# One weight load, two small copies, one scaling and two later steps at the start of a fused RWKV and feed-forward kernel

## The chip, the cores and the metric

The kernel runs on one core of a Trainium2 chip. The metric is the device time of one execution in microseconds (us); the time before is the median of three runs. The engines of the core work side by side, each through its own list of instructions in a fixed order: TensorE (PE, matrix products into the PSUM banks), VectorE (DVE), ScalarE (ACT), GpSimd (POOL) and SyncE (SP). They wait for each other through semaphores. Loads that convert float32 to bfloat16 are issued by POOL and share one software queue; SP and ACT issue others on hardware queues.

## What is computed

A recurrence with a decaying state per head (4 sequences, 8 heads, 768 tokens, head width 48), then a feed-forward layer with a leaky ReLU over all 3072 tokens:

```python
for t in range(S):
    cur = np.einsum('bhd,bhe->bhde', u[None] * kt, vt)
    y[:, :, t] = np.einsum('bhd,bhde->bhe', rt, state + cur)
    state = w[None, :, :, None] * state + np.einsum('bhd,bhe->bhde', kt, vt)
...
h = x @ w_in                      # 384 -> 2048
g = np.maximum(0.01 * h, h)
out = g @ w_out                   # 2048 -> 384
```

## The kernel before

**Tiling.** The tokens are cut into 24 tiles of 128; tile n belongs to sequence n % 4 in a permuted order, so tiles 0 to 3 open the four sequences and have no incoming state. Inside a tile the recurrence is a masked product. Powers of the decay, counted from the middle of the tile, are put into two tables (`qtab` for r, `ktab` for k), so that a scaled r and a scaled k give the weights of all token pairs as one product per head. The state goes from a tile to the next tile of its sequence through `wl`, the decay over 128 tokens.

**Order.** The string `ORDER` (line 29) lists all steps by name; `run` calls them one after the other, and each appends instructions to its engine's list. So the order of two names matters only where both put work on the same engine, where a step reads what another wrote, and where PSUM banks are handed out: `take()` gives the bank that has been free longest in the list's order, `give()` returns one. `Sched` turns the reads and writes of each step into semaphore waits.

**Names used below**, with n the tile:

- Loads: `rn`, `kn`, `vn` are the tile's r, k and v (line 268, POOL, 96 KB in bfloat16); r0 and k0 alone come as float32 over SP and ACT into `r_f` and `k_f` (line 249). `wi0` to `wi3` are the quarters of w_in (line 278, POOL, 384 KB), `wo0` to `wo3` those of w_out (line 282).
- The start: `bc` spreads w over all partitions on PE (line 379, needs the `w_row` load), `lnw`, `qtab`, `ktab` (lines 386, 393, ACT) make the tables; `c0q@`, `c0k@` (line 485, DVE) copy r0 and k0 as bfloat16 into `raw`; `T0q`, `T0k` turn `raw` on PE; `Cu` (line 634, PE) puts w*u by columns into a PSUM bank and `C` (`decay_columns`, line 645) copies it into `wu` in two instructions; `W` (`decay_table`, line 654, ACT) fills `wl` in two instructions.
- A tile: `Pnq`, `Pnk` scale r and k by the tables (`prep_half`, line 431, DVE, into `qk`), `Tnq`, `Tnk` turn them on PE (line 500) and `tnq`, `tnk` bring them back into `tp` on ACT (line 518). `An` is the product for all token pairs (line 529, PE), `Mna`, `Mnb` mask it into `at` on DVE (line 559, from tile 4 on line 563). `Xn` (line 452, DVE) multiplies turned r and k, `Dn` (line 578, PE) sums it with `wu`, `Qn` scales v by that sum (line 459, DVE); from tile 4 on `qn` (lines 466 to 470, DVE) and `Qn` (line 477, POOL) do this in another way. `Yn` (lines 712 and 719, PE) is the tile's output and `yn` (line 733, ACT) copies it into `xT`.
- The state: `Kn` (line 604, PE) is the tile's k-v product, `Sn` (`state`, line 661; line 677 for tiles 0 to 3, DVE) multiplies it by `wl` into the state and gives the bank back.
- The layer: `Gn.f` (line 758, PE) is a quarter of h for tile n, quarter f needing `wif`; `gn.f` (line 769, ACT) is the leaky ReLU; `J`, `j` are the same for two tiles at once; `Hn` (line 782, PE) and `hn` (line 794, ACT) give the output. `F2`, `F4` (line 315) are matmuls whose result nobody reads.

PE's list around the change is: bc, T0q, T0k, Cu, F2, U, A0, T1q, D0, T1k, F4, T3k, K3, A1, D1, Y0, T3q, K0, G0.1, Y1, A3, T2q, D3, G1.1, T2k, G0.3, G1.3, Y3, A2, T4q, T5k, G3.1, G3.3, G3.2, D2, G0.2, T5q, K2, T4k, G1.2.

Of the kernel before, what the change touches and what calls it, by code (L numbers as in the profile page):

```python
# [6 lines left out]
ALU = mybir.AluOpType  # L7
AF = mybir.ActivationFunctionType
# [4 lines left out]
B, H, S, D = 4, 8, 768, 48  # L13
# [5 lines left out]
E = 64  # L19
NP = H // 2  # L20
# [5 lines left out]
TURNED, DIAG, CARRY, EXACT, RAW = 6, 4, 4, 1, 1  # L26
STRIPS = 8
SWAP = 12
ORDER = """
w8 qk0 k0 v0z one r0 trow ones v0y tcol wlz r1 id8 wi1 u8 zr table Cw Wl id E w bc lnw c0q@ T0q c0k@ tri u exps k1 T0k  # L30
u16 wu8 Cu t0q t0k qtab P1q F2 k3 v3 U A0 ktab T1q v0 t1q X0 C D0 P1k T1k t1k F4 M0b P3k M0a T3k K3 utab X1 A1 D1 Q0
Y0 t3k P0k r3 P3q v1 M1a T3q r2 y0 k2 K0 M1b Q1 P2q W G0.1 Y1 t3q X3 wi3 A3 y1 g0.1 S3 T2q D3 G1.1 g1.1 k5 t2q r5 r4
P2k T2k wi2 S0 v2 M3b t2k Q3 G0.3 g0.3 G1.3 k4 M3a Y3 P5k A2 y3 P4q T4q v4 wi0 T5k v5 wo3 t4q g1.3 G3.1 q5 t5k Q5 G3.3
g3.3 P5q r6 wo2 X2 g3.1 M2b wo1 G3.2 D2 Q2 G0.2 g0.2 T5q t5q K2 P4k T4k M2a t4k S2 G1.2 g3.2 q4 Q4 K1 S1 Y2 A5 A4 G1.0
y2 G2.1 M5a G0.0 G2.3 M4a M5b Y5 g0.0 y5 M4b Y4 y4 G2.2 g2.2 K4 J2.4 j2.4 k6 wo0 J2.1 J2.2 g1.0 g1.2 S4 k7 P6q q6 j2.1
P6k P7k G2.0 r7 q7 X6T J2.6 j2.6 J2.3 j2.3 k8 G3.0 J2.7 j2.7 k9 r9 j2.2 J2.5 P7q g3.0 g2.3 X7T J2.0 H1 h1 r8 g2.0 Q6
# [26 lines left out]
class Sched:  # L63
# [7 lines left out]

    def add(self, eng, emit, R=(), W=(), dma=None):
        o = Op()
        o.eng, o.emit, o.dma, o.inc, o.val = eng, emit, dma, False, None
        deps = []
        for key in R:
            w = self.writer.get(key)
            if w is not None:
                deps.append((w, True))
        for key in W:  # L80
            w = self.writer.get(key)
            if w is not None:
                deps.append((w, False))
            for r in self.readers.get(key, ()):
                deps.append((r, False))
        o.deps = []
        for d, raw in deps:
            if d.dma is None and d.eng == eng and dma is None and (eng == "pe" or not raw):
                continue
            if d is not o and d not in o.deps:  # L90
                o.deps.append(d)
        for key in R:
            self.readers.setdefault(key, []).append(o)
        for key in W:
            self.writer[key] = o
            self.readers[key] = []
        self.ops.append(o)
        return o
# [47 lines left out]
def bass_rwkv5_eagle__then__act_leaky_relu_kernel(  # L146
# [13 lines left out]
    def SB(name, shape, dt=BF16):  # L160
        return ctx.enter_context(nc.sbuf_tensor(name, shape, dt))
# [15 lines left out]
    wu = SB("wu", [128, NP, 2])  # L177
    prod = [SB(f"prod{i}", [128, NP, 128]) for i in range(4)]
    lnw = SB("lnw", [128, HD], FP32)
# [3 lines left out]
    qtab = SB("qtab", [128, HD])  # L183
    ktab = SB("ktab", [128, HD])
    tcol = SB("tcol", [128, 1], FP32)
    trow = SB("trow", [128, 2, 128], FP32)
    turned = SB("turned", [128, 2 * NP, 128])
    raw = SB("raw", [128, 2 * H, E])
# [3 lines left out]
    ones = SB("ones", [128, 128])  # L192
# [10 lines left out]
    qk = [SB(f"qk{i}", [128, 2 * H, E]) for i in range(NQK)]  # L203
# [11 lines left out]
    V, A, PE, SP, G = nc.vector, nc.scalar, nc.tensor, nc.sync, nc.gpsimd  # L215
    sch = Sched(ctx, nc)
    add = sch.add
# [6 lines left out]
    def give(key):  # L224
        free.append(key[1])
# [9 lines left out]
    def swapped(n):  # L235
        return n >= SWAP and n % 2 == 0

    def loaded(which, n):
        return [(which, n, 0), (which, n, 1)] if swapped(n) else [(which, n)]
# [11 lines left out]
    def load_one(n, which, pace=()):  # L251
# [6 lines left out]
        if swapped(n):  # L258
# [5 lines left out]
            dst = both.rearrange("p n (h e) -> p (n h) e", h=H)[:, :, 0:D]  # L264
            add("pool", lambda: G.dma_start(dst, src), R=pace, W=[(which, n0, half), (which, n0 + 2, half)],
                dma=f"{which}{n}")
            return
        add("pool", lambda: G.dma_start(dst, src), R=pace, W=[(which, n)], dma=f"{which}{n}")  # L268

# [40 lines left out]
    def fill(n):  # L310
# [7 lines left out]

        add("pe", emit, R=["ones"], W=[("ps", i), f"fill{n}"])

# [101 lines left out]
    def hd(x):  # L422
        return x.rearrange("p (h d) -> p h d", d=D)

    def k_of(n):
        return k_sb[:, slot(n), :] if n >= EXACT else k_f[:, n, :]

    def r_of(n):
        return r_sb[:, slot(n), :] if n >= EXACT else r_f[:, n, :]

    def prep_half(n, half):
        iq = n % NQK
        src, tab, name, done = ((r_of(n), qtab, "r", "qp"), (k_of(n), ktab, "k", "kp"))[half]
        named = "qk"[half] + "tab"
        if swapped(n):
            tab, named = (qtab_s, ktab_s)[half], named + "_s"
        add("dve", lambda: V.tensor_tensor(qk[iq][:, H * half:H * half + H, 0:D], hd(src), hd(tab[:, :]), ALU.mult),  # L437
            R=loaded(name, n) + [named, ("qk0", iq)], W=[(done, iq)])

    def turn_dma(n):  # L440
        iq = n % NQK
# [3 lines left out]
    def prep(n):  # L445
        prep_half(n, 0)
        prep_half(n, 1)
        turn_dma(n)
# [196 lines left out]
    def decay_columns():  # L645
        ps_c, key = c_bank["u"]
        for hh in range(2):
            rows = slice(64 * hh, 64 * hh + D)
            add("dve", lambda rows=rows, hh=hh: V.tensor_copy(
                wu[rows, :, hh:hh + 1].rearrange("p m o -> p (m o)"), ps_c[rows, 0:NP]),  # L650
                R=[key, "wu"], W=[f"wu{hh}"])
        give(key)

# [134 lines left out]
    def g2_out(n, c0=0, c1=HD):  # L788
# [7 lines left out]
        if swapped(n):  # L796
# [12 lines left out]
            W=["w_row"], dma="w"),  # L809
# [7 lines left out]
        "bc": spread_w, "lnw": log_w, "qtab": lambda: table(qtab, tcol, "q", "tcol"),  # L817
        "ktab": lambda: table(ktab, kexp, "k", "kexp"), "Cw": w_columns, "Cu": wu_columns, "E": turned_table,
        "Wl": log_columns, "C": decay_columns, "W": decay_table,
        "u16": u_cast, "U": u_spread, "utab": u_table,  # L820
        "ts": swapped_times, "tris": swapped_triangle,
# [4 lines left out]
    }  # L826
    stage = {
        "P": lambda n, x: prep_half(n, half_of[x]), "T": lambda n, x: turn_mm(n, half_of[x]),
        "t": lambda n, x: turn_out(n, half_of[x[0]], "dve" if x[1:] else "act"),
        "X": lambda n, x: turn_dma(n) if x else diag(n), "A": lambda n, x: a_mm(n), "B": lambda n, x: a_pair(n),  # L830
# [82 lines left out]
```

## Time and profile before

| | |
|---|---|
| median of 3 runs | 167.31 us (166.94 to 167.38) |
| the profiled execution | 166.78 us, its span 165.0 us |
| PE busy | 157.4 us, 95% |
| DVE busy | 105.5 us, 64% |
| ACT busy | 90.4 us, 55% |
| POOL busy | 109.5 us, 66% (issuing loads is counted here) |
| DMA | 20.21 MB, mean 123 GB/s |

Times in the rows below are us from the span's start. A row of the chain of waits gives start, length and the work that set the end; a row of a timeline gives start, length, engine, line, operation, what it writes and reads, how many instructions were merged, and in brackets the idle time before it with what ended it. Instructions of one engine overlap by about 0.1 us in the timelines, so the chain's lengths are the ones to add up. A row of DMA issues ends with the kilobytes and the median us from issue to landing.

### The profile page before, as it was taken

What the parts mean: (1) busy time and instruction counts of PE and PEld (TensorE: products, weight loads), DVE (VectorE), ACT (ScalarE), POOL (GpSimd) and SP (SyncE); (2) the same over time, 40 slices, a digit from 0 to 9 for tenths busy, and PEclk for the clock granted to TensorE, in tenths of its full rate; (3) what the DMA queues carried; (4) which work ended last, traced back from release to release, by engine and by line L of the source; (5) the groups of instructions that cost most, each with busy time, mean ns of one, the idle gap of its engine ahead of it and who ended that gap; (6) DMA issues with size and microseconds to landing.
All of it is one profiled execution on the core that took longest, in us unless ns stands there. A gap on an engine that the chain in (4) does not pass through costs nothing.

```text
span 165.0 us, 5331 instructions
## 1 busy us (share of the span) xinstructions
PE 157.4 (95%) x2303; PEld 119.7 (73%) x2303; DVE 105.5 (64%) x254; ACT 90.4 (55%) x170; POOL 109.5 (66%) x125
## 2 busy tenths in 40 slices
PE   0899999999999999999999999999999999999994
PEld 0487899985568678668668678678678668678663
DVE  7798998269378699948939939939939933000000
ACT  3856883865168339347447447438438439449121
POOL 8999798987999969999199399299380270000000
PEclk9999999999999999999999999999999999999999
DMA  7999999999999999999939959959980630020023
GB/s 110 149 141 158 169 189 190 181 150 154 149 153 202 121 118 137 158 208 130 160 90 113 145 134 94 163 132 81 104 192 4 127 97 3 4 61 34 17 82 97
DMA packets 101365, 20.21 MB, mean 123 GB/s; under 512 B 94555, under 2 KB 101342, under 8 KB 101342
## 3 DMA queue, kind: packets, MB, share of 16 engines
q0 software_dynamic: 76512, 10.03, 93.2%
q1 hardware_dynamic: 23790, 9.65, 29.8%
q8 instruction: 18, 0.29, 0.8%
q10 hardware_dynamic: 1040, 0.20, 0.6%
q14 instruction: 5, 0.04, 0.1%
HBM read 20.45 MB, written 4.72 MB: 153 GB/s over the span
## 4 chain that ended last, share of the span: by engine, by line
PE 91%; ACT 2%; DVE 2%; DMA 2%; SPq 1%; issue 0%; ACTq 0%
PE ps L782 38%; PE ps L758 37%; PE ps L719 6%; PE ps L529 2%; PE ps L500 2%; DMA w_row<-in_w_dram 2%; PE ps L548 1%; PE ps L595 1%; PE ps L604 1%; PE ps L315 1%; ACT xT L733 1%; DVE at L559 1%; PE ps L379 1%; DVE st L677 1%; PE ps L712 1%; ACT out_sb L794 0%
## 5 line engine op out<-in xcount | busy, mean ns | idle before, releaser
L758 PE MATMUL ps<-xT,w_in_sb 128*128 128x256 bf16 (+1 forms) x672 | 66.2, 257 | 0.2
L782 PE MATMUL ps<-w_out_sb,gT 128*128 128x384 bf16 (+2 forms) x400 | 64.6, 320 | 0.0
L769 ACT ACTIVATE gT<-ps 128x512 bf16<-128x512 f32 x96 | 56.3, 598 | 14.8 <-PE ps L758 10.9
L758 PEld LDWEIGHTS ps<-xT,w_in_sb 128*128 128x128 bf16 x672 | 57.2, 98 | 6.6 <-ACT xT L733 0.5
L477 POOL TENSOR_TENSOR at<-ident,s_tok 128x512 bf16<-128x512 bf16 x40 | 42.1, 1081 | 24.8 <-DVE s_tok L470 24.7
L782 PEld LDWEIGHTS ps<-w_out_sb,gT 128*128 128x128 bf16 x400 | 38.1, 98 | 23.1
L794 ACT ACTIVATE out_sb<-ps 128x384 f32<-128x384 f32 (+2 forms) x25 | 11.8, 478 | 45.3 <-PE ps L782 45.3
L563 DVE CAST_PREDICATED at<-mask,ps 128x512 bf16<-128x512 uint16 x28 | 17.8, 685 | 4.7 <-PE ps L529 4.6
L563 DVE CAST_PREDICATED at<-mask_s,ps 128x512 bf16<-128x512 uint16 x12 | 7.7, 687 | 16.1 <-PE ps L548 16.1
L268 POOL DMA_DIRECT2D v_sb<-in_v_dram x18 | 16.3, 920 | 0.0
L268 POOL DMA_DIRECT2D r_sb<-in_r_dram x17 | 15.7, 928 | 0.1
L268 POOL DMA_DIRECT2D k_sb<-in_k_dram x17 | 15.6, 924 | 0.0
L468 DVE TENSOR_TENSOR rku<-r_sb,ku 128x384 bf16<-128x384 bf16 x20 | 12.2, 611 | 0.7
L733 ACT ACTIVATE xT<-ps 128x384 bf16<-128x384 f32 x24 | 10.8, 491 | 2.7 <-PE ps L719 2.6
L470 DVE TENSOR_REDUCE s_tok<-rku 128x8 f32<-128x384 bf16 x20 | 11.1, 553 | 0.7
L719 PE MATMUL ps<-at,v_sb 128*32 128x128 bf16 x384 | 10.8, 223 | 0.0
L719 PEld LDWEIGHTS ps<-tp,st 128*32 128x32 bf16 x240 | 7.2, 96 | 3.0 <-issue 2.9
L719 PEld LDWEIGHTS ps<-at,v_sb 128*32 128x32 bf16 x384 | 8.8, 98 | 0.5 <-issue 0.2
L719 PE MATMUL ps<-tp,st 128*32 128x128 bf16 x240 | 9.1, 221 | 0.0
L671 DVE TENSOR_TENSOR sum_t<-ps,st 64x192 bf16<-64x192 f32 x24 | 8.5, 354 | 0.6
L466 DVE TENSOR_TENSOR ku<-k_sb,u_tab 128x384 bf16<-128x384 bf16 x20 | 7.0, 352 | 2.0 <-DMA k_sb<-in_k_dram 1.8
L437 DVE TENSOR_TENSOR qk<-k_sb,ktab 128x384 bf16<-128x384 bf16 x17 | 7.5, 443 | 1.1 <-DMA k_sb<-in_k_dram 1.0
(82 smaller groups left out, 119.9 us busy)
## 6 DMA issues: line engine op xcount, KB each, us to landing
out_dram<-out_sb SPq DMA_DIRECT2D x17, 192.0 KB, 3.3
v_sb<-in_v_dram POOLq DMA_DIRECT2D x24, 96.0 KB, 5.1
r_sb<-in_r_dram POOLq DMA_DIRECT2D x23, 96.0 KB, 4.5
k_sb<-in_k_dram POOLq DMA_DIRECT2D x23, 96.0 KB, 5.3
w_in_sb<-in_moe_w_in_dram POOLq DMA_DIRECT2D x4, 384.0 KB, 6.3
w_out_sb<-in_moe_w_out_dram POOLq DMA_DIRECT2D x4, 384.0 KB, 7.5
out_dram<-out_sb SPq DMA_DIRECT2D x12, 96.0 KB, 2.2
tp<-qk SPq DMA_TRANSPOSE x18, 4.5
```

Of the source, the lines that this page charges most:

```text
L268: add("pool", lambda: G.dma_start(dst, src), R=pace, W=[(which, n)], dma=f"{which}{n}")
L468: add("dve", lambda: V.tensor_tensor(rku[i2][:, :], r_of(n), ku[i2][:, :], ALU.mult), R=loaded("r", n) + [("ku", i2)], W=[("rku", i2)])
L470: add("dve", lambda: V.tensor_reduce(s_tok[i2][:, :], hd(rku[i2][:, :]), AX.X, ALU.add), R=[("rku", i2)], W=[("s", i2)])
L477: add("pool", lambda hh=hh, s_of=s_of: G.tensor_tensor(at[ia][:, hh, :, :], ident[:, :].unsqueeze(1).to_broadcast([128, NP, 128]), s_of.un ...
L563: add("dve", lambda: V.copy_predicated(at[n % NAT][:, hh, :, :], tri[:, :].bitcast(mybir.dt.uint16).unsqueeze(1).to_broadcast([128, NP, 12 ...
L671: add("dve", lambda part=part: V.tensor_tensor(both[part], kv[part[0]], st[n % NT][part], ALU.add), R=[key, ("st", n % NT)], W=[("sum", n ...
L719: last = PE.matmul(ps_y[32 * q:32 * q + 32, 128 * s:128 * s + 128], a, m, start=not whole and step == 0, stop=step == len(columns[q]) - 1)
L733: add("act", lambda: A.activation(xT[ix][:, :, 128 * slot:128 * slot + 128], ps_y[:, 0:HD].rearrange("p (s t) -> p s t", t=128), AF.Copy), ...
L758: last = PE.matmul(ps_g[:, step * f:step * f + step], w_in_sb[:, s, 128 * fb:128 * fb + 128], xT[ix][:, s, t], start=s == 0, stop=s == NSL ...
L769: add("act", lambda: A.activation(gT[ig][:, fb0:fb0 + count, t], ps_g[:, :].rearrange("p (f t) -> p f t", t=128 * width), AF.Prelu, alpha= ...
L782: last = PE.matmul(ps_o[:, 0:c1 - c0], gT[ig][:, s, 128 * slot:128 * slot + 128], w_out_sb[:, s, c0:c1], start=s == 0, stop=s == NFB - 1)
L794: add("act", lambda: A.activation(out_sb[io][:, c0:c1], ps_o[:, 0:c1 - c0], AF.Copy), R=[key], W=held)
```

## The change

- `wi1` is issued behind `v0` in place of ahead of `k1`, so POOL's list begins r1, k1, k3, v3, v0, wi1, r3 in place of r1, wi1, k1, k3, v3, v0, r3.
- `C` is done by ACT in place of DVE, and stands behind `ktab` in place of behind `X0`; its bank is free that much earlier in the list.
- `P0k` reads k of tile 0 from `raw` (bfloat16) in place of `k_f` (float32).
- `W` stands behind `t3q` in place of ahead of it, on ACT.
- `S0` stands behind `M3a` in place of ahead of `M3b`, on DVE.

The lists of PE and SP keep their order.

```diff
-w8 qk0 k0 v0z one r0 trow ones v0y tcol wlz r1 id8 wi1 u8 zr table Cw Wl id E w bc lnw c0q@ T0q c0k@ tri u exps k1 T0k
-u16 wu8 Cu t0q t0k qtab P1q F2 k3 v3 U A0 ktab T1q v0 t1q X0 C D0 P1k T1k t1k F4 M0b P3k M0a T3k K3 utab X1 A1 D1 Q0
-Y0 t3k P0k r3 P3q v1 M1a T3q r2 y0 k2 K0 M1b Q1 P2q W G0.1 Y1 t3q X3 wi3 A3 y1 g0.1 S3 T2q D3 G1.1 g1.1 k5 t2q r5 r4
-P2k T2k wi2 S0 v2 M3b t2k Q3 G0.3 g0.3 G1.3 k4 M3a Y3 P5k A2 y3 P4q T4q v4 wi0 T5k v5 wo3 t4q g1.3 G3.1 q5 t5k Q5 G3.3
+w8 qk0 k0 v0z one r0 trow ones v0y tcol wlz r1 id8 u8 zr table Cw Wl id E w bc lnw c0q@ T0q c0k@ tri u exps k1 T0k u16
+wu8 Cu t0q t0k qtab P1q F2 k3 v3 U A0 ktab C T1q v0 wi1 t1q X0 D0 P1k T1k t1k F4 M0b P3k M0a T3k K3 utab X1 A1 D1 Q0
+Y0 t3k P0k r3 P3q v1 M1a T3q r2 y0 k2 K0 M1b Q1 P2q G0.1 Y1 t3q W X3 wi3 A3 y1 g0.1 S3 T2q D3 G1.1 g1.1 k5 t2q r5 r4
+P2k T2k wi2 v2 M3b t2k Q3 G0.3 g0.3 G1.3 k4 M3a S0 Y3 P5k A2 y3 P4q T4q v4 wi0 T5k v5 wo3 t4q g1.3 G3.1 q5 t5k Q5 G3.3
...
-        add("dve", lambda: V.tensor_tensor(qk[iq][:, H * half:H * half + H, 0:D], hd(src), hd(tab[:, :]), ALU.mult),
-            R=loaded(name, n) + [named, ("qk0", iq)], W=[(done, iq)])
+        src, reads = (raw[:, H * half:H * half + H, 0:D], [("raw", half)]) if n < RAW else (hd(src), loaded(name, n))
+        add("dve", lambda: V.tensor_tensor(qk[iq][:, H * half:H * half + H, 0:D], src, hd(tab[:, :]), ALU.mult),
+            R=reads + [named, ("qk0", iq)], W=[(done, iq)])
...
-            add("dve", lambda rows=rows, hh=hh: V.tensor_copy(
-                wu[rows, :, hh:hh + 1].rearrange("p m o -> p (m o)"), ps_c[rows, 0:NP]),
+            add("act", lambda rows=rows, hh=hh: A.activation(
+                wu[rows, :, hh:hh + 1].rearrange("p m o -> p (m o)"), ps_c[rows, 0:NP], AF.Copy),
                 R=[key, "wu"], W=[f"wu{hh}"])
```

## The prediction

> **What bounds the kernel now.** I read the page first, then the whole chain of waits, then the timelines of PE, DVE, ACT and POOL over the first 25 us, and last the DMA issues in short windows, one load at a time.
>
> ```profile
> span 165.0 us, 5331 instructions
> ...
> PE 91%; ACT 2%; DVE 2%; DMA 2%; SPq 1%; issue 0%; ACTq 0%
> ```
>
> PE carries the span, so only time in which PE waits can be won, and any new wait of PE is paid in full. All edits lie before 20 us. The chain of waits there:
>
> ```profile
> 5.12 1.01 PE ps L379 x4
> ...
> 12.66 0.58 PE ps L719 x15
> ...
> 13.27 0.49 ACT xT L733
> 13.76 0.24 ACT wl L657
> ...
> 14.41 0.61 ACT tp L518
> ...
> 15.04 0.42 DVE prod L452
> 15.46 0.47 DVE st L677
> 15.93 0.27 DVE qk L437
> 16.20 0.47 DVE st L677
> 16.67 0.60 DVE at L559
> 17.26 0.46 DVE vs L459
> 17.73 0.61 DVE at L559
> ...
> 18.38 0.34 PE ps L712 x3
> 18.73 0.34 PE ps L719 x16
> ...
> 19.94 2.01 PE ps L758 x36
> ...
> 23.21 0.38 PE ps L500 x4
> ```
>
> Three stretches. From 5.12 to 13.24 all pieces are PE's, back to back (the rows left out are PE's too): no other engine can give anything there. From 13.27 to 18.38 the chain leaves PE: y0, W and t3q on ACT, then X3, S3, P2k, S0, M3b, Q3, M3a on DVE, and PE's Y3 starts when M3a ends. From 18.38 on it is PE again, up to the tail.
>
> **The change part by part.** The order of PE's own instructions stays the same; what moves is on POOL, DVE and ACT.
>
> *The two copies of C.* They leave DVE and go to ACT behind ktab:
>
> ```profile
> 4.66 0.17 ACT L642 ACTIVATE wcol<-ps 128x4 f32<-128x4 f32 x1 [2.21 <-PE ps L623]
> ...
> 9.43 1.19 ACT L518 ACTIVATE tp<-ps 128x512 bf16<-128x512 f32 x2 [1.07 <-PE ps L500]
> ```
> ```profile
> 8.58 0.35 DVE L649 CAST wu<-ps 48x4 bf16<-48x4 f32 x2
> ...
> 11.62 0.55 DVE L437 TENSOR_TENSOR qk<-k_f,ktab 128x384 bf16<-128x384 f32 x1
> ...
> 15.85 0.35 DVE L437 TENSOR_TENSOR qk<-k_sb,ktab 128x384 bf16<-128x384 bf16 x1
> ```
>
> ACT's nearest row is L642, the same four columns out of PSUM: 2 x 0.17 = 0.34 us, laid into the 1.07 us that ACT idles before t1q at 9.43. Without that cover t1q, t1k and utab behind it would be 0.34 us late. DVE is freed of 0.35 us. *P0k* reads bfloat16 in place of float32: 0.55 becomes 0.35, as in the bfloat16 row, so 0.20 us less. Both savings, 0.55 us, fall before Y0 at 12.66, in the stretch where PE waits for nobody, and M1a behind them waits for A1 from PE. I take 0; the ends are 0 and, were DVE the limit at y0, -0.55.
>
> *W behind t3q, S0 behind M3a.* T3q ran before y0, so t3q can follow y0 directly: 13.76 to 14.37. X3 needs P2q, over at 14.4: 14.4 to 14.8. W follows t3q with its two instructions, 0.6 to 0.7 us in the chain, to 15.0, well ahead of y1 at 15.2, which waits for Y1 and is not delayed. S3 now waits for W: DVE stands from 14.8 to 15.0 with P2k, M3b, Q3 and M3a queued behind it. From 15.0 the chain's own steps give S3 15.5, P2k 15.75, M3b 16.35, Q3 16.8, M3a 17.4, then S0 17.9 (its bank is asked for next at G3.3, after 20). So M3a ends some 0.9 us earlier than 18.34. PE can't use all of it:
>
> ```profile
> 16.66 1.50 PE L758 MATMUL ps<-xT,w_in_sb 128*128 128x128 bf16 x24
> ```
>
> G0.3 and G1.3 are 24 matmuls of 2.01/36 = 0.056 us: PE is through at 18.0. Y3 moves from 18.38 to 18.0: **-0.38 us at this place**.
>
> *What is late next.* DVE goes on with P5k and P4q; T4q on PE (19.32) needs P4q, T4k (23.21) needs P4k.
>
> ```profile
> 18.24 0.35 DVE L437 TENSOR_TENSOR qk<-k_sb,ktab 128x384 bf16<-128x384 bf16 x1
> 18.68 0.36 DVE L437 TENSOR_TENSOR qk<-r_sb,qtab 128x384 bf16<-128x384 bf16 x1
> ...
> 20.47 1.27 DVE L452 TENSOR_TENSOR prod<-tp 128x512 bf16<-128x512 bf16 x1
> ...
> 22.72 0.34 DVE L437 TENSOR_TENSOR qk<-k_sb,ktab 128x384 bf16<-128x384 bf16 x1
> ```
> ```profile
> 1.41 1.07 POOL L268 DMA_DIRECT2D r_sb<-in_r_dram  x1
> 2.47 0.77 POOL L278 DMA_DIRECT2D w_in_sb<-in_moe_w_in_dram  x1
> 3.20 1.82 POOL L268 DMA_DIRECT2D k_sb<-in_k_dram  x2
> 4.99 1.83 POOL L268 DMA_DIRECT2D v_sb<-in_v_dram  x2
> ...
> 9.41 0.92 POOL L268 DMA_DIRECT2D k_sb<-in_k_dram  x1
> ...
> 11.93 1.78 POOL L268 DMA_DIRECT2D r_sb<-in_r_dram  x2
> ```
>
> The second load of the 11.93 row is r4, issued at 12.8. Its time to landing, and below it those of r1 (issued at 1.41), v0 (5.9), k2 (9.41) and, for comparison, of a load issued at 112.4 in a train on a queue that had been empty:
>
> ```profile
> r_sb<-in_r_dram POOLq DMA_DIRECT2D x1, 96.0 KB, 5.9
> ```
> ```profile
> r_sb<-in_r_dram POOLq DMA_DIRECT2D x1, 96.0 KB, 4.0
> ```
> ```profile
> v_sb<-in_v_dram POOLq DMA_DIRECT2D x1, 96.0 KB, 4.9
> ```
> ```profile
> k_sb<-in_k_dram POOLq DMA_DIRECT2D x1, 96.0 KB, 4.2
> ```
> ```profile
> k_sb<-in_k_dram POOLq DMA_DIRECT2D x1, 96.0 KB, 3.7
> ```
>
> r4 lands at 12.8 + 5.9 = 18.7, and P4q starts at 18.68: **P4q waits for the load already**, if only for the 0.1 us after P5k. From there DVE has no gap to P4k (ku, rku, the reduction, P5q, X2, M2b, Q2, P4k), which ends at 23.06, and PE's T4k starts at 23.21, behind it. So an earlier Y3 is lost again by T4k: if r4 lands when it did, T4k stays at 23.21 and the gain of 0.38 us is worth 0. If r4 is late by d, T4k is late by d, and PE after it has nothing to give it back.
>
> *wi1 behind v0* decides d. All these loads share the software queue, in POOL's order. From v0's landing (10.8) to k2's (13.6) four loads land: 0.70 us each while there is a backlog; POOL issues one in 0.9 us. Before, wi1's big transfer stood second (landed at about 8.1, 2.65 us after r1 at 5.4) and made that backlog at once. After, k1, k3, v3, v0 are issued at 2.47, 3.4, 4.3, 5.2 and wi1 at 6.1, r3 at 6.8 as before. **Lower end:** the queue never runs dry; v0 lands at 5.4 + 4 x 0.70 = 8.2, wi1 at 10.85, where v0 landed before: d = 0. **Upper end:** each lands 3.7 after its issue as at 112.4; v0 at 8.9, wi1 2.65 later at 11.55: d = 0.7. r1's 4.0 is far nearer to 3.7 than to the 4.9 of a backlog, so I take d = 0.5, in the upper half. (wi1 itself, at 11.5, is in time for G0.1 at 13.81; wi3 and wi0 move by d as well and stay ahead of G0.3 and G1.0 until d passes about 0.5 and PE's own delay.)
>
> The Trainium skill, "DMA: Bandwidth & Descriptors", section "Anatomy of one DMA", prices a load of POOL's queue at about 2.0 us plus its bytes over 436 GB/s, 2.2 us for 96 KB. By that rule r4 would be there at 15, the order on the queue would not matter and the 0.38 us would stay won. The trace does not agree: 5.9 us for r4.
>
> **Sum** against the profiled execution (span 165.0, 166.78 us with what lies around it): 0 for C and P0k, -0.38 and +0.38 for W and S0, +0.5 for wi1: 167.3. The median shown, 167.31, is 0.53 above that execution, so the forecast is 167.31 + 0.5 = **167.8 us**, its own range 167.4 to 168.1.
>
> **The rivals.** *r4 stops being late* (the other side). Place: P4q. For it: r4 was late by only 0.1 us, its 5.9 us are 1.7 more than k2's 4.2, and a load that takes the backlog better would be there by 18.4. Then Y3's 0.38 us stay, less what P4q costs: T4q needs it 0.6 us earlier than 19.04. With 0.2 us more from a front that starts earlier because w_row (landed before 5.12) no longer shares the engines with wi1: 167.31 - 0.38 - 0.2 = 166.7. It decides from r4 landing at 18.3 or earlier. Against it: nothing ahead of r4 in the queue gets smaller, only the order changes.
>
> *The queue runs dry at every load.* The train's 3.7 us grow, or POOL's issues stretch as r1's 1.07 did: d of 0.7 to 1.0. wi3 (landed at 10.28 + 5.8 = 16.1 before) then comes after 16.66 too, but that stall and T4k's are one and the same delay: 167.31 + 0.85 = 168.2.
>
> *PE's pace.* The sixteen L719 matmuls take 0.58 at 12.66 and 0.34 at 18.73: PE doubles its pace near 13.2. If the changed stretch moves that point by some 3.4 us, the work between at half pace is worth 1.7 us either way: 165.6 or 169.0. Against it: PE's order and its unbroken stretch from 5.12 stay. The Trainium skill, "TensorE: Matmul & The Clock Gate", Part 1, has the gate judge free-running windows of 3.4 us, by which the phase, not this change, would move it; the halved pace agrees with the rows.
>
> *C on ACT delays D0.* wu is ready at 8.37 + 0.34 = 8.7, D0 runs at 9.19: not given a chance of its own.
>
> **How the numbers follow.** This kernel's measurement tells 0.3%, 0.5 us, from no change: 166.8 to 167.8. Forecast 0.46, its centre on the upper bound: 0.24 slower, 0.22 same. Queue dry at every load 0.26: slower 0.25. r4 in time 0.22: faster 0.16, same 0.06. Pace 0.06: half each side. That is faster 0.19, same 0.29, slower 0.52. The range 166.6 to 168.5 holds the first three cases and leaves out the pace and the tails.
>
> **What would show it.** DVE's row for P4q with an idle ahead of it put down to the r_sb load, at 19.0 to 19.3, and r4's landing 6.2 to 6.5 us after its issue: the forecast's main step. Y3 near 18.0 and M3a's end near 17.4: the W and S0 step. T4q after 19.4 and T4k at 23.5 to 23.9. P0k at 0.35, and the copies on ACT at 0.17 each inside its idle. k1 to v0 landing one every 0.9 us rather than every 0.7 would show the dry queue; 0.7 would refute it. The prediction is wrong if r4 lands at 18.7 or earlier, if T4k starts before 23.2, or if PE's pace doubles elsewhere than at 13.2.

## The result and the profile after

| | before | after |
|---|---|---|
| median in one comparison, 22 runs each | 166.93 us | 167.68 us |
| ratio after/before | | 1.0037, 95% interval 1.0021 to 1.0054 |
| the profiled execution | 166.78 us, span 165.0 us | 166.92 us, span 165.1 us |

The ratio and its interval leave out one far slower execution of each kernel (232.94 us of before, 169.94 us of after). By that ratio the change makes the kernel slower by 0.37%, some 0.6 us (0.0037 x 166.93); the two medians lie 0.75 us apart. The profiled execution of after is one of its fastest: of the 22 runs of after only one, at 166.82 us, is shorter. So its trace shows where the time is decided, but not the whole of the loss.

The chain of waits of after (start, length, what set the end), from the first loads to T4k:

```profile
1.40 1.07 POOL r_sb L268
2.47 1.77 POOL k_sb L268 x2
4.24 1.80 POOL v_sb L268 x2
6.04 0.74 POOL w_in_sb L278
...
11.96 0.82 POOL r_sb L268
12.78 6.10 DMA r_sb<-in_r_dram
...
18.90 0.04 DVE qk L438
...
23.43 0.38 PE ps L501 x4
```

Before, this chain was PE's from 5.12, left it at y0 and came back at Y3 (18.38). Now it is POOL's list of load issues up to 12.78, then r4's 6.10 us to landing, then P4q at 18.90 and DVE without a gap to T4k. Nothing that PE, ACT or DVE does before 18.9 stands in it. T4k starts at 23.43, 0.22 us later than before; behind it the span is the same (165.1 - 23.43 = 141.7 us, before 165.0 - 23.21 = 141.8 us).

The timeline of DVE in after, the rows of P0k, P3q, M3a, S0, P5k and P4q (in brackets the idle time ahead and what ended it):

```profile
11.33 0.35 DVE L438 TENSOR_TENSOR qk<-raw,ktab 128x384 bf16<-128x384 bf16 x1
12.22 0.36 DVE L438 TENSOR_TENSOR qk<-r_sb,qtab 128x384 bf16<-128x384 bf16 x1 [0.54 <-DMA r_sb<-in_r_dram]
...
16.56 0.69 DVE L560 TENSOR_TENSOR at<-ps,mask 128x512 bf16<-128x512 f32 x1
17.16 0.55 DVE L678 TENSOR_TENSOR st<-ps,wl 128x384 bf16<-128x384 f32 x1
17.62 0.35 DVE L438 TENSOR_TENSOR qk<-k_sb,ktab 128x384 bf16<-128x384 bf16 x1
18.90 0.36 DVE L438 TENSOR_TENSOR qk<-r_sb,qtab 128x384 bf16<-128x384 bf16 x1 [0.93 <-DMA r_sb<-in_r_dram]
```

DVE is done with P5k at 17.97, 0.6 us earlier than before, and then stands 0.93 us for r4. It also stands 0.54 us for r3, at P3q.

The timeline of ACT: the two copies of C, t1q and t1k, and W behind t3q; and the timeline of PE: Y0's matmuls, Y3 and T4q:

```profile
8.36 0.35 ACT L650 ACTIVATE wu<-ps 48x4 bf16<-48x4 f32 x2
9.36 1.13 ACT L519 ACTIVATE tp<-ps 128x512 bf16<-128x512 f32 x2 [0.65 <-PE ps L501]
...
13.28 0.59 ACT L519 ACTIVATE tp<-ps 128x512 bf16<-128x512 f32 x1
13.75 0.74 ACT L658 ACTIVATE wl<-wcol 48x192 bf16<-48x192 f32 x2
```
```profile
12.43 0.41 PE L720 MATMUL ps<-at,v_sb 128*32 128x128 bf16 x16
...
17.82 0.33 PE L713 MATMUL ps<-ident,vs 128*128 128x128 bf16 x3
...
19.32 0.62 PE L501 MATMUL ps<-ident,qk 128*128 128x128 bf16 x8 [0.50 <-DVE qk L438]
```

C fills part of ACT's idle time (1.07 us before, 0.65 left). PE takes 0.41 us for the sixteen matmuls of Y0, where before took 0.62, so it doubled its pace near 12.4 in this execution and near 13.2 in before's. It was 0.17 us ahead there besides (12.43, before 12.60), and y0 follows 0.38 us earlier (12.89, before 13.27). Y3 starts at 17.82 in place of 18.38. T4q starts at 19.32, as before: PE finished early and waits 0.50 us for P4q.

The loads, from the view of DMA issues of after, one load at a time (last number: us from issue to landing): k1 (issued at 2.46), v0 (5.06), wi1 (6.03), r3 (6.75), k2 (9.40) and r4 (12.78):

```profile
k_sb<-in_k_dram POOLq DMA_DIRECT2D x1, 96.0 KB, 3.9
...
v_sb<-in_v_dram POOLq DMA_DIRECT2D x1, 96.0 KB, 4.5
...
w_in_sb<-in_moe_w_in_dram POOLq DMA_DIRECT2D x1, 384.0 KB, 5.4
...
r_sb<-in_r_dram POOLq DMA_DIRECT2D x1, 96.0 KB, 5.4
...
k_sb<-in_k_dram POOLq DMA_DIRECT2D x1, 96.0 KB, 4.9
...
r_sb<-in_r_dram POOLq DMA_DIRECT2D x1, 96.0 KB, 6.1
```

Issue and time added give the landing. k1 is there at 6.4 in place of 8.8. But k2 lands at 14.3, where before it landed at 13.6 (9.41 + 4.2): 0.6 us late, with the same loads ahead of it.

What the queue moved meanwhile, from the view of DMA between 8.0 and 8.5 us, first before, then after (packets, MB, mean rate):

```profile
DMA packets 745, 0.07 MB, mean 140 GB/s; under 512 B 745, under 2 KB 745, under 8 KB 745
```
```profile
DMA packets 101, 0.02 MB, mean 39 GB/s; under 512 B 90, under 2 KB 101, under 8 KB 101
```

All these packets are the software queue's. From 4.5 to 8.0 us, with k1 to v0 on it, after moved 105 GB/s; with 96 KB loads in a backlog (8.5 to 11 us) before moved 141. So the queue is short of work in after until wi1 comes, though never without a packet under way.

### The profile page after: what moved, and what is told of

It is laid out like the page before. It is cut to its first block, busy times and chain, and to the rows that moved or that the text cites. A ratio compares the mean times of both kernels' runs of the same rounds, so it can differ in the third digit from the quotient of the medians.

```text
span 165.1 us, 5331 instructions
## 1 busy us (share of the span) xinstructions
PE 157.2 (95%) x2303; PEld 119.6 (72%) x2303; DVE 105.1 (64%) x252; ACT 90.5 (55%) x172; POOL 109.5 (66%) x125
## 4 chain that ended last, share of the span: by engine, by line
PE 84%; POOL 7%; DMA 4%; DVE 2%; ACT 1%; issue 1%; POOLq 0%; ACTq 0%
PE ps L783 38%; PE ps L759 36%; PE ps L720 5%; DMA r_sb<-in_r_dram 4%; POOL r_sb L268 2%; POOL k_sb L268 2%; POOL v_sb L268 2%; PE ps L549 1%; PE ps L530 1%; PE ps L596 1%; POOL w_in_sb L278 1%; DVE prod L453 1%; PE ps L605 1%; ACT xT L734 1%; ACT out_sb L795 0%
## 5 line engine op out<-in xcount | busy, mean ns | idle before, releaser
L770 ACT ACTIVATE gT<-ps 128x512 bf16<-128x512 f32 x96 | 56.3, 598 | 15.0 <-PE ps L759 11.1
L795 ACT ACTIVATE out_sb<-ps 128x384 f32<-128x384 f32 (+2 forms) x25 | 11.8, 478 | 45.3 <-PE ps L783 45.3
L564 DVE CAST_PREDICATED at<-mask,ps 128x512 bf16<-128x512 uint16 x28 | 17.8, 685 | 4.9 <-PE ps L530 4.7
L564 DVE CAST_PREDICATED at<-mask_s,ps 128x512 bf16<-128x512 uint16 x12 | 7.7, 687 | 16.1 <-PE ps L549 16.1
L268 POOL DMA_DIRECT2D r_sb<-in_r_dram x17 | 15.8, 936 | 0.1
L469 DVE TENSOR_TENSOR rku<-r_sb,ku 128x384 bf16<-128x384 bf16 x20 | 12.2, 612 | 0.7
L734 ACT ACTIVATE xT<-ps 128x384 bf16<-128x384 f32 x24 | 10.8, 491 | 2.4 <-PE ps L720 2.3
L471 DVE TENSOR_REDUCE s_tok<-rku 128x8 f32<-128x384 bf16 x20 | 11.1, 553 | 0.7
```

Source lines behind the costliest of these rows:

```text
L469: add("dve", lambda: V.tensor_tensor(rku[i2][:, :], r_of(n), ku[i2][:, :], ALU.mult), R=loaded("r", n) + [("ku", i2)], W=[("rku", i2)])
L471: add("dve", lambda: V.tensor_reduce(s_tok[i2][:, :], hd(rku[i2][:, :]), AX.X, ALU.add), R=[("rku", i2)], W=[("s", i2)])
L564: add("dve", lambda: V.copy_predicated(at[n % NAT][:, hh, :, :], tri[:, :].bitcast(mybir.dt.uint16).unsqueeze(1).to_broadcast([128, NP, 12 ...
L734: add("act", lambda: A.activation(xT[ix][:, :, 128 * slot:128 * slot + 128], ps_y[:, 0:HD].rearrange("p (s t) -> p s t", t=128), AF.Copy), ...
L770: add("act", lambda: A.activation(gT[ig][:, fb0:fb0 + count, t], ps_g[:, :].rearrange("p (f t) -> p f t", t=128 * width), AF.Prelu, alpha= ...
L795: add("act", lambda: A.activation(out_sb[io][:, c0:c1], ps_o[:, 0:c1 - c0], AF.Copy), R=[key], W=held)
```

## The experiments

The theory: moving wi1 leaves the software queue without a backlog while k1 to v0 come in; the time lost there is a delay d of all later loads; r4 is among them and releases P4q. The rivals: the loss belongs to the other four edits (C, P0k, W, S0); r4 stops being late; the queue runs dry at every load; the point at which PE doubles its pace has moved. All edits below that only move names in `ORDER` are shown by the part of the list that they change. Each median stands beside that of the kernel before from the same comparison, in brackets.

**After once more, unchanged.**

> The changed kernel once more, for a second profile. Theory A (the load of r4 is late because w_in's first quarter stands behind v0; P4q waits for it, and all after T4k is late by that): P4q starts at 18.8 to 19.3 behind an idle put down to the r_sb load, T4k at 23.4 to 23.8, time 1.002 to 1.006 of before. Rival B (the copies on ACT, W or S0 cost the time, the loads' order costs nothing): the same time, but T4k no later than before's 23.21 and a wait elsewhere.

Median 167.26 us (before 167.11), ratio 1.0013, interval 0.9987 to 1.0039. Its chain of waits:

```profile
12.79 6.01 DMA r_sb<-in_r_dram
...
23.36 0.38 PE ps L501 x4
```

The chain is the same, with r4 a little earlier. The ratio's interval holds 1 as well as 1.0037: twelve runs don't settle 0.4% here, and the main reading below rests on two kernels, wi1's move alone and the other four edits alone, each measured twice.

**wi1's move alone, twice** (the kernel before, with this edit only):

```diff
-r1 id8 wi1 u8 ... T1q v0 t1q
+r1 id8 u8 ... T1q v0 wi1 t1q
```

> Before, with w_in's first quarter behind v0 and nothing else changed. Theory A: r4 lands at 18.9 (6.1 us after its issue, 5.9 before), P4q starts there, T4k at 23.4 in place of 23.21, time 1.002 to 1.005. Rival B: T4k at 23.2 and time 1.000 within 0.001.

> The same kernel as in the run with w_in's first quarter moved alone, once more, since a single profile scatters: r4 landed at 18.7 to 20.2 in the profiles so far, and T4k came 4.54 us after P4q whenever P4q waited for r4, the end 141.7 us after T4k. Theory A: 1.002 to 1.006 of before again, P4q behind r4. If the first time was scatter: 1.000 within 0.002.

Medians 167.66 us (before 167.11), ratio 1.0044, interval 1.0012 to 1.0075; and 167.62 us (167.14), 1.0032, 1.0009 to 1.0055. The chain of waits of the first, and the timeline of DVE of the second:

```profile
12.78 7.09 DMA r_sb<-in_r_dram
...
19.89 0.04 DVE qk L437
...
24.43 0.38 PE ps L500 x4
```
```profile
13.03 0.36 DVE L437 TENSOR_TENSOR qk<-r_sb,qtab 128x384 bf16<-128x384 bf16 x1 [0.84 <-DMA r_sb<-in_r_dram]
...
19.93 0.36 DVE L437 TENSOR_TENSOR qk<-r_sb,qtab 128x384 bf16<-128x384 bf16 x1 [1.15 <-DMA r_sb<-in_r_dram]
```

The move alone costs as much as the whole change. r4 lands 7.1 us after its issue in both, r3 is late too (P3q stands 0.84 us in the second), and T4k starts 4.54 us behind P4q, as it does in after (23.43 - 18.90 = 4.53). Both profiled executions (168.00 and 168.48 us) are slower than the medians. From 8.0 to 8.5 us the queue moved 44 and 46 GB/s in them, and 89 in after once more.

**The other four edits alone, twice** (after, with wi1 put back):

```diff
-r1 id8 u8 ... T1q v0 wi1 t1q
+r1 id8 wi1 u8 ... T1q v0 t1q
```

> After, with w_in's first quarter back in its old place: C, P0k, W and S0 alone. Theory A: Y3 at 17.8 to 18.0 in place of 18.38, but r4 still lands at 18.7, so DVE idles 0.4 to 0.8 us ahead of P4q, T4k stays at 23.2 and the time at 0.999 to 1.001. Rival B: 1.003 to 1.005, as after. A third way, the gain of 0.38 us stays: 0.997 to 0.998 with T4k at 22.8.

> The same kernel as in the run with all edits but the load, once more. Theory A: 0.998 to 1.001 of before, since r4 (or, ahead of it, k1, which then lands after 8.8) holds DVE and not the steps that became shorter. If those steps gain by themselves: 0.997 or less.

Medians 166.89 us (before 167.11), ratio 0.9998, interval 0.9966 to 1.0029; and 167.01 us (167.14), 0.9991, 0.9961 to 1.0021. C, P0k, W and S0 change nothing that can be measured here (the intervals reach 0.3% to 0.4% to either side). From 8.0 to 8.5 us the queue moved 140 GB/s in both, as in before. The two profiles lie far apart. The chain of waits of the first, then that of the second:

```profile
12.77 7.44 DMA r_sb<-in_r_dram
...
20.24 0.04 DVE qk L438
...
24.78 0.39 PE ps L501 x4
```
```profile
17.06 1.34 PE ps L759 x24
18.40 0.17 PE ps L713 x3
...
22.96 0.36 PE ps L501 x4
```

In the first, r4 took 7.44 us and T4k came at 24.78, later than in after; yet of its 12 runs, the profiled one (168.19 us) is the second slowest, and the median is below before's. In the second, r4 was there at 18.4, P4q waited only 0.15 us for it, and the chain is PE's: T4k at 22.96. One kernel, 1.8 us between two executions: *a single profile of this kernel can't size d.*

The landings of the loads show more. Each is the time of issue (POOL's timeline) plus the time to landing of that load:

| wi1 stands | kernel | v0 | wi1 | r3 | k2 | wi3 | r5 | r4 |
|---|---|---|---|---|---|---|---|---|
| second | before | 10.8 | 8.0 | 11.5 | 13.6 | 16.1 | 18.3 | 18.7 |
| second | the other four edits | 11.1 | 8.3 | 11.8 | 13.9 | 16.8 | 19.6 | 20.2 |
| second | the same, again | 10.8 | 8.0 | 11.5 | 13.6 | 15.5 | 18.0 | 18.4 |
| behind v0 | after | 9.6 | 11.5 | 12.2 | 14.3 | 16.2 | 18.4 | 18.9 |
| behind v0 | after once more | 8.5 | 11.1 | 11.8 | 13.9 | 15.8 | 18.2 | 18.8 |
| behind v0 | wi1's move alone | 9.7 | 12.0 | 12.8 | 14.8 | 16.8 | 19.3 | 19.9 |
| behind v0 | the same, again | 9.1 | 12.3 | 13.0 | 15.6 | 17.6 | 19.0 | 19.9 |
| behind k1 | see below | 11.2 | 9.2 | 12.0 | 14.0 | 16.0 | 18.3 | 18.7 |

Read the table by columns. At k2 the order shows on average: with wi1 second k2 lands at 13.6 to 13.9 (mean 13.7), with wi1 behind v0 at 13.9 to 15.6 (mean 14.6). Single executions can touch: after once more has k2 as early as the latest with wi1 second. Three kernels below have one of these two orders up to k2 as well: before without wi3 has k2 at 14.2; after with r4 ahead of k5 and after without wi3 have it at 15.0 and 14.8. Behind k2 each execution adds something of its own: wi3 lands 1.9 to 2.9 us behind k2, and r5 another 1.4 to 2.9 us behind wi3. That scatter is larger than d, and both end at P4q.

**r4 issued ahead of k5** (after, otherwise unchanged):

```diff
-wi3 A3 y1 g0.1 S3 T2q D3 G1.1 g1.1 k5 t2q r5 r4
+wi3 A3 y1 g0.1 S3 T2q D3 G1.1 g1.1 r4 k5 t2q r5
```

> After, with r4 issued ahead of k5 and r5 in place of behind them. Theory A: r4 lands near 17, P4q follows P5k at about 18.0 with no idle, T4q at 18.8, T4k at 22.6 to 22.9; then w_in's quarter wi0, which lands at 25.2, is the next bound (G1.0 at 25.3 in place of 25.65), so some 0.3 us less than after: 0.999 to 1.001 of before. If r4 is not what holds the stretch: T4k at 23.4 and the time of after, 1.004.

Median 167.31 us (before 167.11), ratio 1.0004, interval 0.9972 to 1.0036. In its chain of waits r4 is gone, but r3 stands there, and PE is slow for long:

```profile
6.75 6.24 DMA r_sb<-in_r_dram
...
17.05 0.54 PE ps L501 x4
...
18.48 0.22 PE ps L501 x4
...
24.61 0.30 PE ps L501 x4
```

Four matmuls of L501 take 0.54 us at 17.05 and 0.22 us at 18.48. So PE doubled its pace between the two, near 17.8 in this execution, where before did it near 13.2, with one and the same order on PE. What r4 gave, r3 and the pace took: T4k at 24.61. The median is what theory A expected, the path is not, and this execution (168.11 us) is the third slowest of its 12.

**wi3 not loaded, in after and in before.** wi3 is struck from `ORDER`, and the products of the fourth quarter read the second quarter's weights in place, so the output is another:

```diff
+at0 = 128 * (fb if fb // 4 != 3 else fb - 8)
...
-R=[("xT", ix, slot) for slot in slots] + [("win", fb0 // 4)],
+R=[("xT", ix, slot) for slot in slots] + [("win", fb0 // 4 if fb0 // 4 != 3 else 1)],
```

> After, without the load of w_in's quarter wi3; its products take quarter 1 instead, so the matmuls are the same in number and size and the output is another. 2.5 us of transfer ahead of r4 and r5 in the queue are gone. Theory A (r4 holds the stretch): r4 lands near 16.4, P4q follows P5k near 18.0 without a wait, T4k moves to 22.5 to 22.8, wi0 lands 2.5 us earlier and holds nothing, time 0.995 to 0.997 of before. If the loads are not the limit: T4k at 23.4, time 1.003.

> Before, without the load of wi3, in the same way. Theory A: r4 is there early, so M3a (18.33) and the rest of DVE's list hold the stretch: P4q at 18.5 to 18.6, T4k at 23.0 to 23.1, time 0.998 to 1.000, so 0.3 to 0.6 us behind the kernel of after without wi3: the gain of C, P0k, W and S0 that the late load hides. If those steps bring nothing by themselves: the same time as after without wi3.

After without wi3: 166.89 us (before 167.07), ratio 0.9998, interval 0.9970 to 1.0027. Before without wi3: 166.85 us, 0.9981, 0.9953 to 1.0010. Neither differs from before, and the gain that was expected did not show. In both the wait for r4 went away, as the timelines of DVE say (the first, P3q and P4q; the second, P1k and P4q):

```profile
12.55 0.36 DVE L438 TENSOR_TENSOR qk<-r_sb,qtab 128x384 bf16<-128x384 bf16 x1 [1.00 <-DMA r_sb<-in_r_dram]
...
18.21 0.36 DVE L438 TENSOR_TENSOR qk<-r_sb,qtab 128x384 bf16<-128x384 bf16 x1
```
```profile
9.33 0.36 DVE L437 TENSOR_TENSOR qk<-k_sb,ktab 128x384 bf16<-128x384 bf16 x1 [0.49 <-DMA k_sb<-in_k_dram]
...
18.87 0.35 DVE L437 TENSOR_TENSOR qk<-r_sb,qtab 128x384 bf16<-128x384 bf16 x1
```

The loads that are late earlier (r3 behind wi1 in the one, k1 behind wi1 in the other) then decide. With 384 KB less on the queue behind it, wi1's place still costs about 1 us of DVE's time at P3q; as a test of r4 the pair is inconclusive.

**r1 issued first** (after, with wi1 put back and r1 ahead of trow):

```diff
-one r0 trow ones v0y tcol wlz r1 id8 u8 ... T1q v0 wi1 t1q
+one r0 r1 trow ones v0y tcol wlz id8 wi1 u8 ... T1q v0 t1q
```

> After, with w_in's first quarter back in its old place and r1 issued ahead of the token rows, at 0.83 in place of 1.41. Theory A: the software queue starts 0.6 us sooner, everything on it lands 0.3 to 0.6 us sooner, r4 near 18.2 where before had 18.65, T4k 0.2 to 0.5 us earlier than in a run of before with the same pace of PE: 0.997 to 0.999. If r4 is not the limit: 1.000, as with the old place alone.

Median 167.32 us (before 167.07), ratio 1.0017, interval 0.9999 to 1.0035: a miss. r1 was issued only 0.15 us earlier (1.25), while every load behind it went out 0.4 us later, and P1k stood for k1. In this execution, the slowest of its 12, the chain again runs through r4, which is issued at 13.17 and lands at 19.69. The wait for k1:

```profile
9.70 0.36 DVE L438 TENSOR_TENSOR qk<-k_sb,ktab 128x384 bf16<-128x384 bf16 x1 [1.05 <-DMA k_sb<-in_k_dram]
```

**wi1 between k1 and k3** (after, otherwise unchanged):

```diff
-exps k1 T0k ... T1q v0 wi1 t1q
+exps k1 wi1 T0k ... T1q v0 t1q
```

> After, with w_in's first quarter between k1 and k3: k1 is early, and the big transfer comes while the queue still has work. Theory A: k1 lands before 7, T1k does not wait, r3 lands near 11.6 to 12.0, r4 as in before (no idle queue ahead of it): 0.998 to 1.001 of before and 0.3% below after. If the queue's dry moments are not what makes r4 late: as after, 1.003.

Median 166.85 us (before 167.14), ratio 0.9981, interval 0.9959 to 1.0003. Its chain of waits:

```profile
12.77 5.89 DMA r_sb<-in_r_dram
...
23.23 0.38 PE ps L501 x4
```

k1 comes early (6.7) and wi1's big transfer still stands in the queue when k3, v3 and v0 arrive, so these land 0.7 us apart and k2 lands at 14.0. The cost of wi1's move is gone from the median: the order of the same loads, not their number, made it. The one profile shows little of this: P4q still waits 0.70 us for r4, and T4k comes 0.2 us earlier than in after.

**The same, with r4 ahead of k5, twice:**

```diff
-exps k1 T0k ... T1q v0 wi1 t1q ... k5 t2q r5 r4
+exps k1 wi1 T0k ... T1q v0 t1q ... r4 k5 t2q r5
```

> As the kernel with w_in's first quarter between k1 and k3, and r4 issued ahead of k5 and r5 as well. Theory A: P4q no longer waits; T4q at 18.8 to 19.2; then r5 (at the reduction of tile 5), wi0 (25.2) or PE's pace holds the end: 0.996 to 0.999 of before. If r4's place does not matter: as the kernel with the load alone.

> The kernel with w_in's first quarter between k1 and k3 and r4 ahead of k5, once more, since its first interval (0.9959 to 1.0001) only touched 1. Theory A: 0.996 to 0.999 of before, P4q right behind P5k near 18.1, the end 141.7 us after T4k. If the first time was scatter: 1.000 or more.

Medians 166.75 us (before 167.14), ratio 0.9980, interval 0.9959 to 1.0001; and 166.82 us (167.00), 0.9982, 0.9967 to 0.9997. This version is 0.2% faster than before; the second interval lies just below 1, the first reaches it. By the ratios to before it is 0.5% faster than after (0.9982/1.0037 = 0.9945), or 0.3% by the second ratio of after (1.0013); the two were not run in one comparison. r4's place adds nothing to wi1's that can be measured: with wi1's alone the ratio was 0.9981. The timeline of DVE of the first shows P4q right behind P5k:

```profile
17.83 0.36 DVE L438 TENSOR_TENSOR qk<-k_sb,ktab 128x384 bf16<-128x384 bf16 x1
18.11 0.35 DVE L438 TENSOR_TENSOR qk<-r_sb,qtab 128x384 bf16<-128x384 bf16 x1
```

T4k starts at 22.64 there and at 22.88 in the second, where P5k waits 0.48 us for k5, which now stands behind r4. The second's chain of waits shows the next bound:

```profile
17.02 8.48 DMA w_in_sb<-in_moe_w_in_dram
...
25.64 1.39 PE ps L759 x22
```

wi0, the last quarter of w_in, lands at 25.5 and PE's G1.0 waits for it, so the span is 165.3 us in spite of the earlier T4k. In this execution, the second slowest of its 12, the queue takes its price one tile further on.

## Why the prediction was right, point by point

**The sum.** 167.8 us was forecast and 167.68 measured. That the totals agree to 0.1 us is partly luck: the base of 167.31, a median of three, was 0.38 us above the 166.93 of the comparison, and the added time of 0.5 us was 0.1 us short by the ratio and 0.25 us short by the medians. The mechanism was right: P4q waits for r4, T4k follows P4q at a fixed distance, and PE gives nothing back. The size of d rests on the medians; the profiled execution shows only 0.2 us of it, those of wi1's move alone 1.2 us. So of the signs that were named, four missed by about 0.1 us in after: r4's time (6.1, not 6.2 to 6.5), P4q (18.90, not 19.0 to 19.3), T4q (19.32, not after 19.4) and T4k (23.43, not 23.5 to 23.9).

**C on ACT, P0k from bfloat16: 0.** Right, with the durations that were taken: 0.35 us for the two copies inside ACT's idle time, 0.35 us for P0k. That the two, with W and S0, are worth less than can be measured is shown by 0.9998 and 0.9991.

**W behind t3q, S0 behind M3a: -0.38 us at Y3, lost again at T4k.** Right that it is lost, and near in size, though in after by another way than the forecast's. Y3 came at 17.82 (18.0 forecast), M3a ended at 17.25 (17.4). But PE, 0.17 us ahead at Y0 and already at the doubled pace, brought y0 0.38 us forward, so W ended at 14.49 and not at 15.0, and S3 (14.76) did not wait for it; M1a to P2q were late instead, behind r3. The forecast's own step, S3 standing 0.2 us for W, is in both executions of the other four edits (0.20 us, at 15.17 and 14.95), where PE doubled its pace near 13.8 and 14.4; there Y3 came at 18.17 and 18.24, earlier than before's 18.38 by 0.14 to 0.21 us only, since PE was through later. The 0.56 us that Y3 gained in after went into PE's wait for P4q, and T4q started at 19.32 as before.

**wi1 behind v0: d = 0.5, between 0 and 0.7.** The term was of the right sign and was mis-sized in how it comes about. The upper end had k1 to v0 each 3.7 us after issue and wi1 at 11.55. k1 to v3 did that (k1 3.9 us in after), which refutes the lower end, 0.70 us apiece. From k1 to v0 the loads landed 0.8 to 1.2 us apart on average in the four executions, which is the sign named for a dry queue. But v0 came later still in three of four executions (9.1 to 9.7, against 8.9), and wi1 at 11.1 to 12.3. At k2 the delay against before was 0.2 to 2.0 us, not 0 to 0.7. By r4 part of it was caught up in after: wi3 landed 1.9 us behind k2, where before took 2.5. The forecast took the time between k2 and r4 as fixed; it varies by more than d (4.3 to 6.3 us).

**r3 and k5.** The prediction's late load was r4 alone. r3 stands behind wi1 too, and P3q waited for it in after (0.54 us) and in both runs of wi1's move alone (0.60 and 0.84 us). It cost nothing where r4 came later still; it decided where r4 had been taken away. k5, ahead of r4 on the queue, held P5k for 0.69 us in after once more and 0.76 us in the first run of wi1's move alone. These steps were missing.

**The rivals.** *r4 stops being late* is refuted: with wi1 behind v0, r4 landed at 18.8 to 19.9 in the four executions of the table, never by 18.3. The earlier front that this rival counted on (0.2 us) doesn't follow wi1: L379 starts at 4.89 to 5.08 with wi1 behind v0, and at 5.12, 5.03 and 4.99 with wi1 second. *The queue dry at every load* is nearer than its chance said: the profiled executions of wi1's move alone have T4k 1.2 us later than before (24.43 and, in the second, 24.47). Their medians, at 1.0044 and 1.0032, are 0.7 and 0.5 us above before's, between this rival's 0.85 and the forecast's 0.5. Its late wi3 is there too in the second: wi3 lands at 17.59, and G0.3 starts behind it at 17.63. *PE's pace* does move: PE doubled it near 13.2 in before and near 12.4 in after, which the prediction had named as a sign that it is wrong. It cost nothing here: where P4q waits for r4 it is hidden, since r4's issue at 12.8 does not depend on PE. The point also moves between executions of one kernel: near 12.4 and 11.6 in the two of after, 13.8 and 14.4 in the two of the other four edits, with one order on PE. The granted clock reads 1.00 from 0 to 25 us in before, after and the run with r4 ahead of k5, so only the matmuls' spacing shows the doubling (107, then 56 ns between starts in the last). Its moving from execution to execution agrees with the Trainium skill, "TensorE: Matmul & The Clock Gate", Part 1, by which the gate's windows run freely and the number of slow matmuls varies from run to run; no run here separates the phase from the load.

**What stays open.** Why v0 and wi1 land up to 0.8 us later than the upper end in some executions and 0.4 to 0.5 us earlier in another; how much of the cost goes through r4 alone, since with r4 out of the way r3, k5, wi0 or PE's pace decided; and whether the other four edits win back part of wi1's cost, which the ratio of 1.0013 in the second comparison allows and 1.0037 in the first doesn't show.

## What to carry to other kernels

On a queue whose loads are issued more slowly than they are served (here 0.9 us against 0.7 us for 96 KB), a large transfer early in the order is worth something in itself: the small loads behind it arrive as a backlog and land one after the other, while the same transfer put behind them leaves the queue short of work first (39 in place of 140 GB/s at 8 us here) and then holds up all that follows. Where the chain of waits ends in a load, look along the queue for the load that sets the delay, and don't count time won on the engines until that load is earlier. Where a kernel's executions scatter by more than the effect, settle the size by many timed runs of the edit alone and of its complement, and use profiles for the place.

## What the runs showed of the hardware

r4's time to landing ranged from 5.6 to 7.4 us for one order of loads (before and the two runs with the other four edits). The hold-up falls between wi3 and r5: three loads of 96 KB, k5, r5 and r4, follow wi3 and elsewhere land some 0.7 us apart, but k5 lands 2.2 us behind wi3 in after once more, and r5 1.4 us behind k5 in after. In the view of DMA issues, after's k5 and r5 (issued at 11.00 and 11.92):

```profile
k_sb<-in_k_dram POOLq DMA_DIRECT2D x1, 96.0 KB, 6.0
...
r_sb<-in_r_dram POOLq DMA_DIRECT2D x1, 96.0 KB, 6.5
```

In seven of the eight traces of the table one of these gaps is 1.4 to 2.3 us wide; in the second run of wi1's move alone none reaches 1 us. In all eight, one transfer of 0.02 MB on the queue named "instruction" lies between 15.5 and 17.5, within about 1 us of the start of that gap where there is one. For before, between 16.0 and 16.5 (name, packets, MB, share of 16 engines):

```profile
q8 instruction: 1, 0.02, 12.2%
```

12.2% of 16 engines over 0.5 us is 0.98 us on one engine (0.122 x 16 x 0.5). Whether it holds up the loads was not tried.

Of the 96 KB loads up to r4 in those eight traces the quickest landed 3.5 us after its issue, and r1, with nothing ahead of it on the queue, took 4.0 us in before. The rule of the Trainium skill's "DMA: Bandwidth & Descriptors", section "Anatomy of one DMA", that the prediction weighed against r4 gives 2.2 us, and so misses the smallest of these too.
